# Eight opening loads handed to two queues by turns, in a fused adaLN attention and gMLP block

## The chip, the cores and the metric

One NeuronCore of one Trainium2 chip runs the whole program. The time is the device time of one execution, in microseconds (us); for each kernel the median of several executions is given. One further execution was taken with the hardware profiler, and all views of the trace belong to that one.

## The reference

The block has 2048 tokens of width 448, 16 heads of width 28, and a gMLP of inner width 896. Cut to what matters:

```python
mod = (silu(c) @ w_mod)                      # c is 1 x 448, w_mod is 448 x 2688
sa, ca, ga, sb, cb, gb = six rows of 448
h = layernorm(x) * (1 + ca) + sa
q, k, v = h @ wqkv                           # 448 x 1344
x = x + ga * (softmax(q k^T * 28**-0.5) v @ wo)
h = layernorm(x) * (1 + cb) + sb
z = gelu(h @ w_in); z1, z2 = z[:, :896], layernorm(z[:, 896:])
x = x + gb * ((z1 * (w_sp @ z2 + b_sp)) @ w_out)
```

Everything is in float32; nothing can be projected before `sa` and `ca` are there, and these need `silu(c)` and a third of `w_mod`.

## The kernel before, in words

The order on each engine is written out by hand: every engine runs its instructions strictly in the order in which the program issues them, and semaphores tie the engines together. The change lies in the first stage, the projections.

**The opening.** Tokens come in four groups of 512 (`load_x`, four tiles of 128 tokens each; line 175). Group 0 is loaded in three transfers (tile 0, tile 1, tiles 2 and 3), the others in one. `load_mod` (line 170) loads the first third of `w_mod`, the part for `sa` and `ca`, as four blocks of 112 rows, here called wm0 to wm3. `load_w("v", i)` loads the 448 rows of V's weights in blocks 0, 2, 1 (line 186) and 3; block 3 is 64 rows, loaded twice into the two halves of one tile (lines 87 and 88). So the opening's transfers stand in this order: c (line 202), three of x, wm0 to wm3, V's five, then group 1 of x. All of them are issued by SyncE (SP). ScalarE (ACT) issues transfers in one place only, the last stage, where it stores the output (line 1252).

**Completion counters.** The framework gives each transfer one of eight completion counters, by turns, in program order and over both issuing engines together. A transfer whose counter was used before waits, on the engine that issues it, until the earlier transfer with that counter has landed. The ninth transfer so waits for the first, the tenth for the second, and so on. The instruction that waits holds what stands behind it on its engine.

**What the first instructions do.** ACT loads its function table and computes `exp(-c)` into `ec` (line 214). VectorE (DVE) makes `silu` of it (lines 215 to 217). Behind these stand DVE's layer norm statistics of tiles 0 and 1 (lines 273, 274), their normalisation (284, after GpSimd's `rs`, lines 107 and 108), the statistics of tiles 2 and 3, then `mod_acc`: wm0 times its column of `silu` (233), wm1 added (235), the normalisation of tiles 2 and 3, wm2 added (235). `mod_last` (385) adds wm3 a column block at a time, TensorE (PE) sums over the rows (`pc`, line 391), and DVE writes the columns of `ca` and `sa` (397). With these ACT and DVE make the modulated, transposed h (409, 404, 84), and PE multiplies it with V's weights (`pv`, line 300). PE transposes the normalised tiles at line 351. Short matmuls that compute nothing (`pe_fill`, line 224) stand around those, to keep PE busy.

The first part of the weights of q and k (`load_w("a", i)`, lines 186, 87, 88) reuses the four buffers of wm0 to wm3. Later stages are attention (lines 572 to 618), the output projection, the gMLP's first matmul, the token mixing and the last matmul.

Of the kernel before, what the change touches and what calls it, by code (L numbers as in the profile page):

```python
# [33 lines left out]
def tile_adaln_mha_gmlp(ctx, tc, x, wqkv, wo, w_in, w_spT, b_sp, w_out, cT, w_mod, out):  # L34
    nc = tc.nc
    ctx.enter_context(tc.manual_schedule())
    pe, dve, act, pool, sp = nc.tensor, nc.vector, nc.scalar, nc.gpsimd, nc.sync
# [48 lines left out]
    def load_z(eng, dst, src):  # L86
        eng.dma_start(dst[0:64], src)
        eng.dma_start(dst[64:128], src)
# [73 lines left out]
    wms, xts, raws = {}, {}, {}  # L162
# [4 lines left out]
    def load_mod(pair, eng):  # L167
        for k in range(4):
            wms[pair, k] = e1.tile([112, 2, D], F32, name="wm", tag=("wm", "wm", "raw")[pair], bufs=4)
            eng.dma_start(wms[pair, k], w_mod[:, pair, k])  # L170

    def load_x(g, eng):
        xg = e1.tile([128, 4, D], F32, name="xg")
        for t0, t1 in ((0, 1), (1, 2), (2, 4)) if g == 0 else ((0, 4),):
            eng.dma_start(xg[:, t0:t1, :], x[g, :, t0:t1])
        for t in range(4):
            xts[4 * g + t] = xg[:, t, :]

# [3 lines left out]
    def load_w(kind, i, eng):  # L182
        c0, n, tag = PARTS[kind]
        raw = e1.tile([128, 2 * D], F32, name="raw", tag=tag, bufs=4)[:, :n]
        if i < 3:
            eng.dma_start(raw, wqkv[i * 128 : (i + 1) * 128, c0 : c0 + n])
        else:
            load_z(eng, raw, wqkv[384:448, c0 : c0 + n])
        raws[kind, i] = raw
# [11 lines left out]
    cc_t = e1.tile([112, 4], F32, name="cc_t", bufs=1)  # L201
    sp.dma_start(cc_t, cT)
    load_x(0, sp)
    load_mod(0, sp)
    for i in (0, 2, 1, 3):
        load_w("v", i, sp)
    load_x(1, sp)
    pool.memset(wv[64:128, 7, :].bitcast(F32), 0.0)
    pool.memset(wqk[64:128, 7, 0:896].bitcast(F32), 0.0)
# [240 lines left out]
    h_lo(3, dve)  # L450
    wv_lo(3, pool)
    load_x(2, sp)
    for i in (0, 2, 1, 3):
        load_w("b", i, sp)
# [7 lines left out]
    for i in (0, 2):  # L462
        qk_lo("a", i, dve)
    load_mod(1, sp)
    for a in pvs:
        v_copy(*a)
# [25 lines left out]
    for i in (0, 2, 1, 3):  # L492
        qk_part("b", i, dve)
    load_mod(2, sp)
    for g in range(1, NG):
        if g == 3:
# [878 lines left out]
```

## Time and profile before

| what | value |
|---|---|
| median of 3 executions | 1408.03 us (1407.81 to 1408.63) |
| the profiled execution | 1407.25 us |
| its span, first to last instruction | 1405.5 us |
| granted TensorE clock | 1.00 |
| DVE, ACT and GpSimd busy | 72%, 56%, 21% of the span |
| transfers issued by SP (queue q1) and by ACT (queue q10) | 181.88 MB and 3.84 MB |

The page of the profile gives the busy time of each engine, the span in 40 equal slices, the transfers, and the chain of work that ended last. The timeline gives single instructions: start, duration, engine, line, and in brackets how long the engine stood idle before it and what ended that. SPq and ACTq are the instructions by which SP and ACT issue transfers. Such an instruction is shown from the end of its wait on.

### The profile page before, as it was taken

Reading aid. Unit: us, or ns where it says so; the run is one execution under the profiler, and the core shown is the slowest. Engines: PE = TensorE matmul, PEld = TensorE weight load, DVE = VectorE, ACT = ScalarE, POOL = GpSimd, SP = SyncE. Lnnn points to the kernel's source line nnn. Section 1 sums busy time; section 2 is a strip of 40 time slices with the busy share of each in tenths; the row PEclk is TensorE's granted clock in tenths of the full one; section 3 lists DMA queues with packets and bytes.
Section 4 is the critical chain, followed back from the end, with each engine's and each line's share of the span. In section 5 each row is a group of like instructions: output and inputs, shape, how many; then the busy total and the mean of one; then the engine's idle time right before and its main releaser. Section 6 shows DMA issues by size and latency. Waiting matters only on the chain.

```text
span 1405.5 us, 20321 instructions
## 1 busy us (share of the span) xinstructions
PE 1393.3 (99%) x7164; PEld 981.2 (70%) x7164; DVE 1014.1 (72%) x1701; ACT 788.9 (56%) x1536; POOL 296.3 (21%) x284
## 2 busy tenths in 40 slices
PE   7999999999999999999999999999999999999999
PEld 7887655555555555555555554988998888888888
DVE  7798888888888888888888860751356655668574
ACT  4723677777777777777677779263234544434211
POOL 4234313122314243313200021100143430001000
PEclk9999999999999999999999999999999999999999
DMA  8564645555455556654422001534103333444453
GB/s 256 156 169 168 187 110 171 167 161 157 154 167 171 150 164 179 178 158 150 123 68 75 21 18 45 187 115 139 53 0 113 107 113 111 142 140 157 142 174 108
DMA packets 99377, 187.01 MB, mean 133 GB/s; under 512 B 17736, under 2 KB 29130, under 8 KB 96730
## 3 DMA queue, kind: packets, MB, share of 16 engines
q1 hardware_dynamic: 96846, 181.88, 43.0%
q10 hardware_dynamic: 2430, 3.84, 0.7%
q8 instruction: 56, 0.92, 0.3%
q14 instruction: 45, 0.37, 0.1%
HBM read 130.42 MB, written 50.46 MB: 129 GB/s over the span
## 4 chain that ended last, share of the span: by engine, by line
PE 96%; DMA 2%; DVE 1%; ACT 0%; issue 0%; SPq 0%; POOL 0%; DVEq 0%; ACTq 0%; POOLq 0%
PE st_ps L603 19%; PE o_ps L618 17%; PE mt L572 17%; PE acc L1143 6%; PE acc L1142 6%; PE acc L1144 6%; PE z_ps L1068 5%; PE z_ps L954 5%; PE pq L318 5%; PE wo_ps L824 3%; PE pv L300 2%; PE y_ps L1247 2%; PE y_ps L1248 2%; PE y_ps L1246 2%; PE tp L117 1%; DMA wm<-in_w_mod_dram 1%
## 5 line engine op out<-in xcount | busy, mean ns | idle before, releaser
L577 DVE TENSOR_REDUCE pm<-mt 128x1 f32<-128x512 f32 x1024 | 631.5, 682 | 110.0 <-PE mt L572 109.8
L607 ACT ACTIVATE P<-st_ps 128x512 f32<-128x512 f32 x1024 | 513.2, 621 | 150.0 <-PE st_ps L603 150.0
L603 PE MATMUL st_ps<-qst,kst 128*128 128x512 f32 x1024 | 407.5, 409 | 0.1
L572 PE MATMUL mt<-kst,qst 128*128 128x512 f32 x1024 | 402.1, 393 | 0.6 <-DVE pm L577 0.3
L603 PEld LDWEIGHTS st_ps<-qst,kst 128*128 128x128 f32 x1024 | 191.1, 187 | 151.4 <-issue 82.2
L618 PE MATMUL o_ps<-P,V 128*32 128x512 f32 x2048 | 247.5, 598 | 0.0
L572 PEld LDWEIGHTS mt<-kst,qst 128*128 128x128 f32 x1024 | 192.5, 188 | 32.9 <-DVE pm L577 2.3
L725 POOL TENSOR_TENSOR ws_raw<-ws_raw 128x512 f32<-128x512 f32 x80 | 102.9, 1287 | 282.8 <-DMA ws_raw<-in_w_spT_dram 270.4
L1030 ACT ACTIVATE wsp_h<-raw_sp 128x512 fp32r<-128x512 f32 x112 | 69.9, 631 | 154.4 <-PE acc L1144 103.6
L84 DVE TENSOR_TENSOR wsp_l<-raw_sp,wsp_h 128x512 fp32r<-128x512 f32 x112 | 82.0, 743 | 81.9 <-ACT wsp_h L1030 81.2
L618 PEld LDWEIGHTS o_ps<-P,V 128*32 128x32 f32 x2048 | 54.1, 109 | 123.5 <-issue 116.6
L1143 PE MATMUL acc<-wsp_l,heapA 128*128 128x512 f32 x224 | 87.4, 390 | 0.3 <-DVE wsp_l L84 0.2
L1142 PE MATMUL acc<-wsp_h,heapA 128*128 128x512 f32 x224 | 87.3, 390 | 0.0
L1144 PE MATMUL acc<-wsp_h,heapA 128*128 128x512 f32 x224 | 87.2, 389 | 0.0
L1143 PE MATMUL acc<-wsp_l,heapB 128*128 128x512 f32 x174 | 67.7, 389 | 0.0
L1144 PE MATMUL acc<-wsp_h,heapB 128*128 128x512 f32 x174 | 67.7, 389 | 0.0
L1142 PE MATMUL acc<-wsp_h,heapB 128*128 128x512 f32 x174 | 67.7, 389 | 0.0
L318 PE MATMUL pq<-heapD,heapD 128*128 128x512 f32 x196 | 61.9, 390 | 0.0
L1072 DVE BATCH_NORM_STATS2 stz<-z 128x6 f32<-128x448 f32 x32 | 19.9, 625 | 50.4 <-ACT z L1071 30.1
L1143 PEld LDWEIGHTS acc<-wsp_l,heapA 128*128 128x128 f32 x224 | 42.0, 188 | 9.6 <-DVE wsp_l L84 1.2
L1142 PEld LDWEIGHTS acc<-wsp_h,heapA 128*128 128x128 f32 x224 | 42.0, 188 | 9.0 <-DVE cD L1148 0.3
L1144 PEld LDWEIGHTS acc<-wsp_h,heapA 128*128 128x128 f32 x224 | 42.0, 188 | 8.8
(212 smaller groups left out, 1605.7 us busy)
## 6 DMA issues: line engine op xcount, KB each, us to landing
ws_raw<-in_w_spT_dram SPq DMA_DIRECT2D x160, 256.0 KB
ws_scr<-ws_raw SPq DMA_DIRECT2D x80, 256.0 KB
raw_sp<-ws_scr SPq DMA_DIRECT2D x80, 256.0 KB
kst<-qk_scr SPq DMA_DIRECT2D x45, 224.0 KB
qst<-qk_scr SPq DMA_DIRECT2D x45, 224.0 KB
raw_sp<-in_w_spT_dram SPq DMA_DIRECT2D x32, 256.0 KB
qk_scr<-qh SPq DMA_DIRECT2D x28, 256.0 KB
qk_scr<-ql SPq DMA_DIRECT2D x28, 256.0 KB
```

Source lines behind the costliest of these rows:

```text
L84: eng.tensor_tensor(out=dst, in0=a, in1=hi.bitcast(F32), op=ALU.subtract)
L318: pe.matmul(pq, wqk[:, b, m * 128 : (m + 1) * 128], hT[g][:, a, :], start=j == 0, stop=j == NST - 1)
L572: pe.matmul(mt, qst[h % 3][:, t * 128 : (t + 1) * 128], kst[h % 3][:, kb * 512 : (kb + 1) * 512], start=True, stop=True)
L577: dve.tensor_reduce(out=pms[h][:, t, kb : kb + 1], in_=mt, axis=AX.X, op=ALU.max)
L603: pe.matmul(st, kst[h % 3][:, kt * 128 : (kt + 1) * 128], qst[h % 3][:, qb * 512 : (qb + 1) * 512], start=True, stop=True)
L607: act.activation(p, st, AF.Exp, scale=SCALE)
L618: pe.matmul(otile[h][32 * qb : 32 * qb + 32, :], V[:, kt, h, :], ptiles.pop((u, qb)), start=kt == 0, stop=kt == NT - 1)
L725: pool.tensor_tensor(out=a, in0=a, in1=b, op=SUMS[i // 16][2])
L954: pe.matmul(ps_t, w1[:, b, f * 128 : (f + 1) * 128], h2T[g][:, a, :], start=j == 0, stop=j == NST - 1)
L1142: pe.matmul(acc[i], zh, hi, start=st == 0, stop=False)
L1143: pe.matmul(acc[i], zh, lo, start=False, stop=False)
L1144: pe.matmul(acc[i], zl, hi, start=False, stop=st == 7)
```

## The change

Every second transfer of the opening gets ACT as its issuing engine: tile 1 of x, wm0, wm2, and V's blocks 2 and 3 (six transfers, since block 3 has two). c, tile 0, tiles 2 and 3, wm1, wm3, V's blocks 0 and 1 and group 1 of x stay with SP. Line numbers stay as they are.

```diff
     def load_mod(pair, eng):
         for k in range(4):
...
-            eng.dma_start(wms[pair, k], w_mod[:, pair, k])
+            (act if pair == 0 and k % 2 == 0 else eng).dma_start(wms[pair, k], w_mod[:, pair, k])
     def load_x(g, eng):
...
-            eng.dma_start(xg[:, t0:t1, :], x[g, :, t0:t1])
+            (act if t0 == 1 else eng).dma_start(xg[:, t0:t1, :], x[g, :, t0:t1])
...
     for i in (0, 2, 1, 3):
-        load_w("v", i, sp)
+        load_w("v", i, act if i in (2, 3) else sp)
```

In the built program the order on PE, DVE and GpSimd is the same as before. ACT's program begins with the six transfers, and the table load and `exp(-c)` come behind them. The counters are given out in the same turns, over both engines in the order in which they issue. On ACT, tile 1, wm0 and wm2 wait for nothing; V's block 2 waits until c has landed, the first half of block 3 until wm0 has, and its second half until wm1 has, which SP issues.

## The prediction

> **What bounds the kernel now.** I read the page first, then busy time by stretch, then the chain of work that ended last in the first 70 us, then the engines' timelines there. From the page:
>
> ```profile
> PE 1393.3 (99%) x7164; PEld 981.2 (70%) x7164; DVE 1014.1 (72%) x1701; ACT 788.9 (56%) x1536; POOL 296.3 (21%) x284
> ```
>
> The busy times from 26 us up to the last 55 (window, length, busy time of PE, PEld, DVE, ACT, POOL, granted clock, DMA share, GB/s):
>
> ```profile
> 26.00:1350.00 1324.00, 1322.94 (x6804) 917.61 (x6805) 963.13 (x1607) 770.77 (x1503) 284.94 (x267) 1.00 0.43 130
> ```
>
> The reader is to see that from 26 us on PE never pauses: 1322.9 us of 1324. Nothing later can take in a delay. What shifts PE's start at 26 us shifts the end by as much, and nothing else in this change moves the end. So the question is the first 26 us. Their chain (start, duration, what):
>
> ```profile
> 4.00 10.50 DMA wm<-in_w_mod_dram
> ...
> 26.06 1.89 PE pv L300 x8
> ```
>
> The chain names wm3's transfer, but DVE's timeline says how much that transfer really costs:
>
> ```profile
> 2.62 1.01 DVE L215 TENSOR_SCALAR ec<-ec 112x4 f32<-112x4 f32 x1 [1.49 <-ACT ec L214]
> 3.67 0.18 DVE L216 RECIPROCAL ec<-ec 112x4 f32<-112x4 f32 x1
> 3.88 0.16 DVE L217 TENSOR_TENSOR silu<-cc_t,ec 112x4 f32<-112x4 f32 x1
> 4.33 0.63 DVE L273 BATCH_NORM_STATS2 st<-xg 128x6 f32<-128x448 f32 x1 [0.30 <-DMA xg<-in_x_dram]
> ...
> 11.19 1.15 DVE L235 SCALAR_TENSOR_TENSOR acc<-wm,silu,acc 112x896 f32<-112x896 f32 x1 [0.94 <-DMA wm<-in_w_mod_dram]
> ...
> 14.59 1.66 DVE L385 SCALAR_TENSOR_TENSOR acc<-wm,silu,acc 112x128 f32<-112x128 f32 x6 [0.34 <-DMA wm<-in_w_mod_dram]
> ...
> 17.69 0.16 DVE L397 TENSOR_SCALAR col_ca<-pc 128x1 f32<-128x1 f32 x1 [0.45 <-PE pc L391]
> ```
>
> From 4.33 us to 26 us DVE runs one chain, up to the parts of h that the `pv` at 26.06 needs. It waits for transfers only three times: 0.30, 0.94 and 0.34 us, 1.58 us in all. That is everything that earlier landings could ever give back. And the chain's head is `silu`, which waits for ACT's `ec`.
>
> **The change part by part.** *ACT's queue.* ACT's start before:
>
> ```profile
> 0.71 1.28 ACT L214 ACT_TABLE_LOAD   x1 [0.71 <-PEq L1363]
> 2.39 0.20 ACT L214 ACTIVATE ec<-cc_t 112x4 f32<-112x4 f32 x1 [0.39 <-DMA cc_t<-in_cT_dram]
> ```
>
> Now six issues stand ahead of both, and the last waits until wm1 has landed. Whether such a wait holds ACT's own work is shown where ACT issues transfers today, at the end:
>
> ```profile
> 1359.37 0.34 ACTq L1252 DMA_DIRECT2D out_dram<-x2l  x1
> 1359.75 1.68 ACT L1218 ACTIVATE uT<-cE 128x512 fp32r<-128x512 f32 x3 [8.15 <-DVE x2l L1251]
> ```
>
> ACT stood idle for 8.15 us until the issue's own input was there, and its next activation came behind it. So `ec` comes when wm1 has landed, the issue is out, and the table is loaded. Behind `ec` stands DVE's whole chain, and behind that PE.
>
> *When wm1 lands.* SP's timeline tells of landings, because each issue from the ninth on waits for one (8.10: all of group 0 of x; 9.44: wm0; 11.10: wm1; 12.93: wm2; DVE's row at 14.59: wm3):
>
> ```profile
> 1.18 1.36 SPq L175 DMA_DIRECT2D xg<-in_x_dram  x3
> 2.59 1.91 SPq L170 DMA_DIRECT2D wm<-in_w_mod_dram  x4
> ...
> 8.10 0.56 SPq L87 DMA_DIRECT2D raw<-in_wqkv_dram  x1
> 9.44 0.47 SPq L88 DMA_DIRECT2D raw<-in_wqkv_dram  x1
> 11.10 0.33 SPq L175 DMA_DIRECT2D xg<-in_x_dram  x1
> 12.93 2.75 SPq L186 DMA_DIRECT2D raw<-in_wqkv_dram  x3
> ```
>
> The four w_mod issues were out by 4.50 us, 10 us before wm3 landed, so these landings are set by bytes, not by issuing. The 16 DMA engines are full, as the same view by stretch shows:
>
> ```profile
> 0.00:2.00 2.00, 0.00 (x0) 0.00 (x0) 0.32 (x3) 1.28 (x1) 1.34 (x8) 1.00 0.03 1
> ...
> 7.00:13.00 6.00, 4.23 (x31) 4.04 (x30) 4.82 (x10) 0.71 (x3) 1.32 (x3) 1.00 1.03 237
> 18.00:20.00 2.00, 2.00 (x11) 1.86 (x10) 2.00 (x4) 1.57 (x3) 0.22 (x1) 1.00 1.05 381
> ```
>
> Sizes, from the list of issues:
>
> ```profile
> wm<-in_w_mod_dram SPq DMA_DIRECT2D x12, 392.0 KB
> raw<-in_wqkv_dram SPq DMA_DIRECT2D x3, 224.0 KB
> xg<-in_x_dram SPq DMA_DIRECT2D x2, 224.0 KB
> xg<-in_x_dram SPq DMA_DIRECT2D x1, 448.0 KB
> ```
>
> After the change wm1 is the last of 224 + 448 + 392 = 1064 KB on SP's queue. ACT's queue meanwhile carries 224 + 2 x 392 = 1008 KB (tile 1, wm0, wm2) and then 224 KB of V's block 2, which need c alone. If the engines serve both queues in turn, 2072 to 2296 KB are through when wm1 is. Before, 2072 KB (x and wm0 to wm2) were through at 12.9 us and 392 KB more at 14.55, so 2296 KB would be at 13.85. ACT can issue tile 1 from 0.71 us on (its row above), where SP issued its first tile of x at 1.18, so the first rows of x start 0.47 us earlier: 12.4 to 13.4 us. I take 12.8. So wm1, which before came second of four, now lands where wm2 did. The bound from below: all 2072 KB (2.12 MB) at the best of these rates, 381 GB/s, take 5.6 us. Before, almost nothing moved until 2.0 us; from 0.47 us sooner on that gives 7.1 us. From above: wm3's old place, 14.6.
>
> The page "DMA: Bandwidth & Descriptors" of the Trainium skill ("Issuing engines are not separate DMA queues") says that transfers from several engines run on the same 16 DMA engines and interleave, and that only issue time is saved. The share of 1.03 in the row above agrees with it; no row here shows two queues loading at once. By that page the 7.1 us would fall away as a bound.
>
> *From there to DVE.* The last issue takes 0.47 us (the row at 9.44) from 12.85 to 13.32, the table load 1.28 to 14.65, `ec` 0.20 to 14.87. DVE's first step took 1.01 us, because it ended with a GpSimd memset:
>
> ```profile
> 2.65 0.96 POOL L210 MEMSET V<- 128x1024 f32 x1
> ```
>
> That is long over now, so I take 0.16 us, as the small operation of line 397 has in the row at 17.69; bounds 0.16 and 1.01. The two steps to `silu` and the gaps take 0.46 as before (3.63 to 4.09). The statistics start at 15.5 instead of 4.33: **+11.2 us**. wm0 to wm3 have landed when they are asked for, so the waits of 0.94 and 0.34 go: **-1.3 us**. What is late next is PE's share in that chain:
>
> ```profile
> 4.98 4.08 PE L224 MATMUL wu<-ones,xg 128*128 128x128 f32 x18 [4.98 <-DVE st L273]
> 8.90 1.04 PE L351 MATMUL tp<-ident,xn 128*128 128x128 f32 x8
> 9.77 1.28 PE L224 MATMUL wu<-ones,xg 128*128 128x128 f32 x10
> 12.82 1.09 PE L351 MATMUL tp<-ident,xn 128*128 128x128 f32 x8 [1.77 <-DVE xn L284]
> ```
>
> The first 18 fills take 3.92 us up to the next row, 0.22 each; the transposes behind them 0.11, later fills 0.13. The fills wait for x alone, so they still run at 4 to 8 us, and then PE stands idle some 12 us until tile 0 is normalised. If it comes back at the slow pace, the 8 transposes and 10 fills, 18 matmuls too, take 3.9 us instead of 2.1. They start at 20.1 (8.90 + 11.2) and end at 24.0; the next transposes could start at 23.1 (12.82 + 11.2 - 0.94). So these come 0.9 later, and DVE's wait of 0.45 for the last `pc` grows by about **+0.7**. Bounds 0 and 0.9; I take 0.7, since the only long idle time in the trace, the start, was followed by the slow pace. By the Trainium skill's page "TensorE: Matmul & The Clock Gate" (Part 1), an idle time over about 3.4 us halves the clock; no later pause here shows it, and by that rule the 0.7 stands.
>
> *What stays hidden.* V's block 3 lands near 15 us and is used behind 28. Group 1 of x is now issued when tiles 2 and 3 have landed, but stands behind wm3 and V's blocks on SP's queue. The q and k weights still wait for wm0's to wm3's buffers, which come free about 10 us later, but then meet empty queues. Their earlier landing gives nothing (0 to -0.03), since DVE was busy for 7.97 of the last 8 us:
>
> ```profile
> 18.00:26.00 8.00, 7.36 (x35) 6.12 (x33) 7.97 (x9) 4.54 (x8) 6.22 (x5) 1.00 0.99 320
> ```
>
> SP's shorter queue gives nothing, since its issues waited for landings.
>
> **Sum:** 11.2 - 1.3 + 0.7 = +10.6 us, on the profiled execution (1407.25 us, span 1405.5) 1417.85, on the median, 0.78 above it, **1418.6 us** (+0.75%).
>
> **The rivals.** *Two queues move more bytes.* DMA engines that serve two queues might overlap them and reach 381 GB/s at once; then wm1 lands at 7.1 us and the loss is 10.6 - 5.7 = 4.9: 1412.9. For it: that rate is reached at 18 us, with one queue. Against: the share is already 1.03 with one.
>
> *wm1 lands last.* If ACT's rows are served first, wm1 waits for most of them and lands at wm3's old 14.6: +1.8, 1420.4 (1420.5 in the range, for the median's own spread).
>
> *Not slower: the wait stands in ACT's queue of transfers and not in ACT.* If ACT could go on to the table and `ec` while an issue waits, `silu` would come in time and earlier landings could remove the three waits: 1408.03 - 1.58 = 1406.4. It decides at `ec`: for no loss, `ec` must end by about 5.0 us (`silu` by 4.04 + 1.58, less 0.16 + 0.46). With ACT blocked that would need wm1 landed by 2.9 us, when it has barely been issued. The rows at 1359 us speak against it.
>
> **How the numbers follow.** Forecast 0.70, more bytes 0.17, wm1 last 0.08, not slower 0.05. The range runs from the first rival's time to the second's, 1412.9 to 1420.5. About 0.2% (2.8 us) is what a measurement can tell from no change. Not even the best case gains so much: faster 0.01, same 0.05, slower 0.94.
>
> **What would show it.** Right: ACT's table load near 13.4 us, behind six issues, of which the last two stand behind waits until about 9 and 12.8 us; DVE's `ec` idle 13 us or so; statistics at 15.5; no wait for wm; `pv` first at about 28; PE without a pause from 37. Wrong: a table load before 5 us, or a `pv` start that moves less than `silu` does.

## The result and the profile after

| what | before | after |
|---|---|---|
| median of 6 executions of each | 1407.91 us (1407.68 to 1408.63) | 1417.07 us (1416.90 to 1419.76) |
| ratio, after to before | | 1.0065, 95% interval 1.0054 to 1.0077 |
| the profiled execution, its span | 1407.25, 1405.5 us | 1417.01, 1415.2 us |

The changed kernel is 9.2 us slower. From the page of after, the busy times; and from its busy time by stretch, the row for 36 us up to the last stages (window, length, busy time of PE, PEld, DVE, ACT, POOL, granted clock, DMA share, GB/s):

```profile
PE 1396.3 (99%) x7164; PEld 983.5 (69%) x7164; DVE 1013.2 (72%) x1701; ACT 788.6 (56%) x1536; POOL 295.1 (21%) x284
```

```profile
36.00:1350.00 1314.00, 1312.63 (x6749) 907.45 (x6748) 953.92 (x1590) 768.83 (x1500) 281.76 (x266) 1.00 0.43 130
```

PE again never pauses once its long run has begun, now from about 36 us on. So the first 36 us are the place to look. ACT's timeline of after (start, duration, instruction, idle time before it and what ended that):

```profile
0.72 0.43 ACTq L175 DMA_DIRECT2D xg<-in_x_dram  x1
1.18 0.92 ACTq L170 DMA_DIRECT2D wm<-in_w_mod_dram  x2
3.06 0.35 ACTq L186 DMA_DIRECT2D raw<-in_wqkv_dram  x1
6.07 0.56 ACTq L87 DMA_DIRECT2D raw<-in_wqkv_dram  x1
10.98 0.48 ACTq L88 DMA_DIRECT2D raw<-in_wqkv_dram  x1
11.49 1.28 ACT L214 ACT_TABLE_LOAD   x1 [11.49 <-DMA raw<-in_wqkv_dram]
12.79 0.20 ACT L214 ACTIVATE ec<-cc_t 112x4 f32<-112x4 f32 x1
```

Six issues, then the table load, then `ec`. The last two issues stand behind waits, until 6.07 and 10.98. The bracket names `raw`, V's block 2, of which a piece came in at 11.44; but the table load starts 0.03 us after the last issue ends, and what held that issue until 10.98 is named by the chain of work that ended last:

```profile
2.12 8.84 DMA wm<-in_w_mod_dram
10.98 0.48 ACTq L88
11.49 1.28 ACT L214
...
34.55 1.90 PE pv L300 x8
```

The transfer that SP issued from 2.12 us on is wm1, and it landed at 10.96. DVE's timeline of after, with the same instructions as those shown of before:

```profile
13.03 0.17 DVE L215 TENSOR_SCALAR ec<-ec 112x4 f32<-112x4 f32 x1 [11.89 <-ACT ec L214]
...
13.52 0.62 DVE L273 BATCH_NORM_STATS2 st<-xg 128x6 f32<-128x448 f32 x1
...
19.27 1.15 DVE L235 SCALAR_TENSOR_TENSOR acc<-wm,silu,acc 112x896 f32<-112x896 f32 x1
21.03 0.94 DVE L284 TENSOR_SCALAR xn<-xg,mv,rs 128x448 f32<-128x448 f32 x2 [0.61 <-POOL rs L108]
...
23.06 1.67 DVE L385 SCALAR_TENSOR_TENSOR acc<-wm,silu,acc 112x128 f32<-112x128 f32 x6
...
26.16 0.16 DVE L397 TENSOR_SCALAR col_ca<-pc 128x1 f32<-128x1 f32 x1 [0.44 <-PE pc L391]
```

The statistics start at 13.52 instead of 4.33: **+9.19 us**. From there to `mod_last` (line 385) it is 9.54 us instead of 10.26: the waits of 0.94 and 0.34 for wm are gone, but a new one of 0.61 for GpSimd's `rs` has come: **-0.72 us**. PE's timeline of after:

```profile
16.82 1.97 PE L351 MATMUL tp<-ident,xn 128*128 128x128 f32 x8 [9.03 <-DVE xn L284]
18.57 2.34 PE L224 MATMUL wu<-ones,xg 128*128 128x128 f32 x10
21.60 1.10 PE L351 MATMUL tp<-ident,xn 128*128 128x128 f32 x8 [0.68 <-DVE xn L284]
...
34.55 1.90 PE L300 MATMUL pv<-wv,heapD 128*128 128x448 f32 x8 [0.57 <-DVE heapD L84]
```

The last `pv` of the stage starts at 34.55 instead of 26.06, +8.49, which the two DVE terms give (9.19 - 0.72 = 8.47). The profiled executions differ by 9.76 in all, and the medians by 9.16. What is beyond the stage, 0.7 to 1.3 us, comes up bit by bit later, where both kernels do the same work: DVE runs the same 1701 instructions in the same order, and they are 8.5 us late at 128 us of before, 10.7 at 804 us, near the end of attention, and 9.8 at the end. The kernel before itself ran from 1405.87 to 1412.02 us in 24 executions on one chip. So the shift of this `pv` is the sharper measure, and the experiments use it as "the stage's shift", beside the medians.

### The profile page after: what moved, and what is told of

Same layout as the page of the kernel before. It is cut to its first block, busy times and chain, and to the rows that moved or that the text cites. A ratio compares the mean times of both kernels' runs of the same rounds, so it can differ in the third digit from the quotient of the medians.

```text
span 1415.2 us, 20321 instructions
## 1 busy us (share of the span) xinstructions
PE 1396.3 (99%) x7164; PEld 983.5 (69%) x7164; DVE 1013.2 (72%) x1701; ACT 788.6 (56%) x1536; POOL 295.1 (21%) x284
## 4 chain that ended last, share of the span: by engine, by line
PE 96%; DVE 2%; DMA 1%; POOL 0%; ACT 0%; issue 0%; SPq 0%; ACTq 0%; DVEq 0%; POOLq 0%
PE st_ps L603 19%; PE o_ps L618 17%; PE mt L572 17%; PE acc L1143 6%; PE acc L1144 6%; PE acc L1142 6%; PE z_ps L1068 5%; PE z_ps L954 5%; PE pq L318 5%; PE wo_ps L824 3%; PE pv L300 2%; PE y_ps L1247 2%; PE y_ps L1248 2%; PE y_ps L1246 2%; PE tp L117 1%; DMA wm<-in_w_mod_dram 1%
```

## The experiments

Three theories stood against each other. **A**: the loss is the wait for a landing that stands in ACT's program ahead of the table load and `ec`. **B**: two queues loading at once make the transfers land later where they are needed. **C**: it is the time that ACT spends on issuing. Each edit is shown against the changed kernel, except where it says otherwise. The ratio in the table is an estimate from all executions, with its interval; it can differ from the quotient of the two medians by up to 0.0007.

| kernel | ACT issues | start of tile 0's statistics | stage's shift | median, its kernel before | ratio (95%) |
|---|---|---|---|---|---|
| after | all six | 13.52 | +8.49 | 1417.07, 1407.91 | 1.0065 (1.0054 to 1.0077) |
| e1_x_wm | tile 1, wm0, wm2 | 5.29 | +0.25 | 1410.38, 1408.59 | 1.0006 (0.9996 to 1.0017) |
| e2_v_only | V's three | 14.25 | +11.22 | 1418.11, 1408.59 | 1.0060 (1.0045 to 1.0076) |
| e3_last_half_sp | all but the last | 8.60 | +3.55 | 1412.13, 1408.59 | 1.0020 (1.0011 to 1.0029) |
| e4_ec_first | all six, behind `ec` | 4.10 | +3.34 | 1412.62, 1408.59 | 1.0025 (1.0015 to 1.0035) |
| e5_warm | all six, more fills | 14.03 | +12.46 | 1419.28, 1407.27 | 1.0083 (1.0069 to 1.0096) |
| e6_wait_alone | none | 10.32 | +5.27 | 1415.84, 1407.27 | 1.0056 (1.0038 to 1.0073) |
| e7_v_only_warm | V's three, more fills | 14.32 | +9.27 | 1416.93, 1407.27 | 1.0068 (1.0052 to 1.0083) |
| e8_ec_then_wm | wm0, wm2, behind `ec` | 4.36 | +4.21 | 1412.73, 1407.27 | 1.0036 (1.0023 to 1.0048) |

The two-queue part without a wait on ACT, **e1_x_wm**:

```diff
-        load_w("v", i, act if i in (2, 3) else sp)
+        load_w("v", i, sp)
```

> ACT issues tile 1 of x, wm0 and wm2, which wait for nothing; all of V's weights are SP's again. Theory A (the loss is ACT's wait for landings in its own program, ahead of exp(-c)): three issues end near 2.1 us, the table load near 3.4, ec near 3.65; the first statistics start when tile 0 of x lands, near 5.4, DVE then has no wait for wm, and the wm3 step starts at 14.4 against 14.59 before: about -0.2 us, a time of 1407.7, within 1 us of before. Rival B (two queues at once make the loads land later or hold each other up, and that is the loss): x and wm still come by two queues, so most of the loss stays, +6 to +9 us. Rival C (the loss is the issue time on ACT, 0.45 us each, and the table load behind it): +1.5 us.

ACT's and DVE's timelines of e1_x_wm:

```profile
1.18 0.92 ACTq L170 DMA_DIRECT2D wm<-in_w_mod_dram  x2
2.13 1.28 ACT L214 ACT_TABLE_LOAD   x1 [2.13 <-issue]
3.43 0.20 ACT L214 ACTIVATE ec<-cc_t 112x4 f32<-112x4 f32 x1
```

```profile
5.29 0.63 DVE L273 BATCH_NORM_STATS2 st<-xg 128x6 f32<-128x448 f32 x1 [1.04 <-DMA xg<-in_x_dram]
...
12.81 0.93 DVE L284 TENSOR_SCALAR xn<-xg,mv,rs 128x448 f32<-128x448 f32 x2 [0.61 <-POOL rs L108]
```

And the last `pv` of the stage, from PE's:

```profile
26.31 1.89 PE L300 MATMUL pv<-wv,heapD 128*128 128x448 f32 x8 [0.55 <-DVE heapD L84]
```

Three issues that wait for nothing delay `ec` by only 1.04 us (3.43 instead of 2.39), and `silu` (4.08, 0.16 long) is still there before the first tile of x. The statistics of tile 0 start 0.96 later than before, now that tile 1 and wm0 load beside that tile; the waits for wm are gone, the one for `rs` is there: +0.96 - 0.72 = +0.24, and the `pv` moved by +0.25. Two queues and 1.4 us of issuing on ACT cost nothing that the executions can tell: the interval of the ratio holds 1, though the medians lie 1.8 us apart, where less than 1 was expected. B and C fall as the cause of 8.5 us.

V's part alone, **e2_v_only**:

```diff
-            (act if pair == 0 and k % 2 == 0 else eng).dma_start(wms[pair, k], w_mod[:, pair, k])
+            eng.dma_start(wms[pair, k], w_mod[:, pair, k])
...
-            (act if t0 == 1 else eng).dma_start(xg[:, t0:t1, :], x[g, :, t0:t1])
+            eng.dma_start(xg[:, t0:t1, :], x[g, :, t0:t1])
```

> Only V's blocks 2 and 3 are issued by ACT; x and wm come by SP's queue alone, as before. Their counters make ACT wait for tile 0 of x, for tiles 2 and 3, and last for wm1. Theory A: wm1 lands at 11.1 as before, ec ends near 13.2, the statistics start near 13.8, the wm3 step near 23.2: +8.7 us in that stage, a time near 1416.6 to 1417. Rival B: nothing is loaded by two queues before wm3 is through, so no loss, 1408. Rival C: three issues and the table load, +1.5 us.

ACT's timeline of e2_v_only, then PE's and DVE's:

```profile
11.70 0.49 ACTq L88 DMA_DIRECT2D raw<-in_wqkv_dram  x1
12.22 1.28 ACT L214 ACT_TABLE_LOAD   x1 [12.22 <-DMA raw<-in_wqkv_dram]
```

```profile
22.33 1.97 PE L351 MATMUL tp<-ident,xn 128*128 128x128 f32 x8 [0.68 <-DVE xn L284]
```

```profile
26.68 0.16 DVE L397 TENSOR_SCALAR col_ca<-pc 128x1 f32<-128x1 f32 x1 [1.22 <-PE pc L391]
```

The wait is all here, with no x or w_mod issued by ACT: the statistics come 9.92 late, which with the -0.72 is +9.20. The stage moved by 11.22, so 2.0 us are new. They are PE's: its second eight transposes take 1.97 us here and 1.10 in after, and DVE waits 1.22 us for the first `pc`, a wait that after doesn't have. The term that the prediction put at +0.7 exists, and is larger, in this kernel.

The same transfers with one wait less on ACT, **e3_last_half_sp** (the second half of block 3 goes to SP, so ACT's last wait is the one for wm0):

```diff
     def load_z(eng, dst, src):
         eng.dma_start(dst[0:64], src)
-        eng.dma_start(dst[64:128], src)
+        (sp if eng is act else eng).dma_start(dst[64:128], src)
```

> As the changed kernel, but the second half of V's block 3 is issued by SP, so that the last landing for which ACT waits is wm0's (6.05 us in the trace of after) and not wm1's (10.96). Theory A: ACT's last issue ends at 6.6, the table load at 7.9, ec at 8.15, the statistics start at 8.7 instead of 13.5; waits for wm are still gone, GpSimd's second step is still late by 0.6: +3.7 us against before, 1411.6. Rival B: nothing changes in the two queues' loads, so +9 as in the changed kernel. Rival C: one issue less, +8.5.

ACT's and DVE's timelines of e3_last_half_sp:

```profile
5.98 0.56 ACTq L87 DMA_DIRECT2D raw<-in_wqkv_dram  x1
6.57 1.28 ACT L214 ACT_TABLE_LOAD   x1 [6.57 <-DMA wm<-in_w_mod_dram]
```

```profile
8.60 0.62 DVE L273 BATCH_NORM_STATS2 st<-xg 128x6 f32<-128x448 f32 x1
```

The table load follows the landing of wm0 as it followed that of wm1. 8.60 - 4.33 - 0.72 = 3.55, and the stage moved by 3.55. One issue of 0.48 us, moved to the other engine, is worth 4.9 us, since the wait for wm1 went with it.

All six issues behind the work that they held up, **e4_ec_first**:

```diff
     sp.dma_start(cc_t, cT)
+    ec = e1.tile([112, 4], F32, name="ec", bufs=1)
+    act.activation(ec, cc_t, AF.Exp, scale=-1.0)
     load_x(0, sp)
...
-    ec = e1.tile([112, 4], F32, name="ec", bufs=1)
-    act.activation(ec, cc_t, AF.Exp, scale=-1.0)
```

> As the changed kernel, all six transfers by ACT, but the table load and exp(-c) are issued ahead of them. Theory A: silu comes as before, DVE's chain runs as before; ACT still stands at the wait for wm1 until about 11 us, so the two small copies for the transposes, due at 7.6, come near 11.6, PE's transposes follow, and DVE's wait for the last pc grows from 0.45 by some 0.7: +0.5 to +1 us, about 1408.6. Rival B: the two queues carry the same loads, so +6 to +9 us. Rival C: the issues no longer stand ahead of ec, 0.

ACT's issue of tile 1 and DVE's statistics of tiles 0 and 1, from the timeline of e4_ec_first:

```profile
2.42 0.44 ACTq L175 DMA_DIRECT2D xg<-in_x_dram  x1
```

```profile
4.10 0.63 DVE L273 BATCH_NORM_STATS2 st<-xg 128x6 f32<-128x448 f32 x1
9.10 0.63 DVE L273 BATCH_NORM_STATS2 st<-xg 128x6 f32<-128x448 f32 x1 [4.16 <-DMA xg<-in_x_dram]
```

`silu` is in time again, and 5.2 of the 8.5 us are back. That is less than expected: tile 1 is issued 2.42 us into the run, when SP has already issued tiles 2 and 3 and is issuing w_mod, and it lands only at 9.08. DVE stands 4.16 us for it. Theory B, wrong for the changed kernel, is right here: what is needed first shares the engines with what is needed later.

The clock, by more fills, so that PE doesn't stand still while it waits for tile 0, **e5_warm**:

```diff
-    pe_fill(9, x1)
+    pe_fill(48, x1)
```

> The changed kernel with 48 instead of 9 fills ahead of the transposes, so that PE works on from 3.6 to about 16.5 us and its clock stays up. The prediction's third term (the slow pace costs 0.7 us): the last pv group of tiles 0 to 3 (34.55 us in after) starts 0.7 earlier, near 33.85. What the trace of after says against it (DVE's wait for the last pc is 0.44, before 0.45): no move, 34.55 within 0.1.

PE's timeline of e5_warm, then a row of its busy time by stretch (the third number from the end is the granted clock):

```profile
3.67 13.76 PE L224 MATMUL wu<-ones,xg 128*128 128x128 f32 x96 [3.67 <-DMA xg<-in_x_dram]
...
22.11 1.09 PE L351 MATMUL tp<-ident,xn 128*128 128x128 f32 x8 [2.57 <-DVE xn L284]
```

```profile
23.00:24.00 1.00, 1.00 (x8) 1.00 (x7) 0.96 (x3) 0.70 (x2) 0.00 (x0) 0.60 0.25 92
```

This missed: it was 4.0 us worse than after in the stage. 0.5 of that is the start of the statistics (wm1 landed at 11.47 here). The rest is the clock: it stayed full through the first transposes, where speed is worth nothing, and halved at 23.2 us, behind the later pause of 2.57 us, just ahead of `pc` and `pv`; it was 0.50 until 33.4. So the clock matters by where the slow microseconds fall.

The wait without anything else, **e6_wait_alone**: the kernel before, all transfers on SP, the table load at the start, and one tiny activation that reads wm1 ahead of `ec`. Its output is used nowhere. The edit is against the kernel before, and later lines move down by two.

```diff
     ec = e1.tile([112, 4], F32, name="ec", bufs=1)
+    seen = e1.tile([112, 4], F32, name="seen", bufs=1)
+    act.activation(seen, wms[0, 1][:, 0, 0:4], AF.Copy)
     act.activation(ec, cc_t, AF.Exp, scale=-1.0)
```

> The kernel before, all transfers by SP, with one small activation ahead of exp(-c) that reads four columns of wm1: ACT waits for wm1 by data, not by a counter, and no second queue loads anything. The table load stays at the start. Theory A (the wait ahead of exp(-c) is the loss): wm1 lands at 11.1, ec ends at 11.55, the statistics start at 12.1; with the wm waits gone (-1.3) and GpSimd's second step late by 0.6 the stage loses 7.0 us, and up to 2 more if PE's clock comes back late: 1415 to 1417. Rival B (two queues at once) and rival C (ACT's issue time): 0, 1408.

ACT's, SP's, DVE's and PE's timelines of e6_wait_alone:

```profile
9.49 0.20 ACT L215 ACTIVATE seen<-wm 112x4 f32<-112x4 f32 x1 [7.49 <-DMA wm<-in_w_mod_dram]
```

```profile
9.48 0.34 SPq L175 DMA_DIRECT2D xg<-in_x_dram  x1
```

```profile
10.32 0.62 DVE L275 BATCH_NORM_STATS2 st<-xg 128x6 f32<-128x448 f32 x1
```

```profile
31.33 1.89 PE L302 MATMUL pv<-wv,heapD 128*128 128x448 f32 x8 [0.57 <-DVE heapD L84]
```

Under B and C this edit costs nothing. It costs 10.32 - 4.33 - 0.72 = 5.27 us by the stage's sum, and the stage moved by 5.27. It is less than the 7.0 expected, because wm1 landed at 9.46 in this profile, where the same transfers in the same order landed it just before 11.10 in the profile of before (SP's row there). The size goes with the landing, as A says. The median moved by more than the stage (8.6 us, interval 5.3 to 10.3): the profiled execution is the shortest of four, 1411.57 us at a mean granted clock of 1.000, and the others took 1415.78 to 1418.77 at 0.998 to 0.995. Where in these the clock was lower, no trace shows.

The clock in e2, by the same means as in e5, **e7_v_only_warm**:

```diff
     # against e2_v_only
-    pe_fill(9, x1)
+    pe_fill(46, x1)
```

> The run with only V's blocks 2 and 3 by ACT, with 46 instead of 9 fills, so that PE works on until its transposes. There the last pv group of tiles 0 to 3 started at 37.28, and from DVE's wm3 step to the first pv it took 4.93 us against 2.92 in after, with the granted clock at 0.50 until 26.9. If the clock is the cause: 2.92 again, the last pv group near 35.3, the stage's loss 9.2 instead of 11.2. If something else in that run held PE: no move.

PE's timeline of e7_v_only_warm:

```profile
22.40 1.09 PE L351 MATMUL tp<-ident,xn 128*128 128x128 f32 x8 [2.34 <-DVE xn L284]
...
35.33 1.89 PE L300 MATMUL pv<-wv,heapD 128*128 128x448 f32 x8 [0.56 <-DVE heapD L84]
```

The statistics start where e2's do (14.32 and 14.25), the transposes take 1.09 us instead of 1.97, and the stage's shift falls from 11.22 to 9.27. 14.32 - 4.33 - 0.72 = 9.27: nothing is left over. The 2.0 us of e2 were PE's pace.

`ec` first, and only w_mod by two queues, **e8_ec_then_wm** (wm0 and wm2 by ACT, behind `ec`; x and V by SP):

```diff
     sp.dma_start(cc_t, cT)
+    ec = e1.tile([112, 4], F32, name="ec", bufs=1)
+    act.activation(ec, cc_t, AF.Exp, scale=-1.0)
...
-            (act if t0 == 1 else eng).dma_start(xg[:, t0:t1, :], x[g, :, t0:t1])
+            eng.dma_start(xg[:, t0:t1, :], x[g, :, t0:t1])
...
-        load_w("v", i, act if i in (2, 3) else sp)
+        load_w("v", i, sp)
...
-    ec = e1.tile([112, 4], F32, name="ec", bufs=1)
-    act.activation(ec, cc_t, AF.Exp, scale=-1.0)
```

> A candidate: table load and exp(-c) stay first on ACT, then ACT issues wm0 and wm2 alone; x, wm1, wm3 and all of V's weights stay with SP. No wait stands on ACT. Theory A: silu as before, tile 0 lands near 4.1, wm1 and wm3 land before DVE asks; of the 1.58 us of waits 0.2, 0.34 and 0.94 less 0.61 (GpSimd's second step takes its place) go: the last pv group of tiles 0 to 3 near 25.2 instead of 26.06, -0.9 us, which the times can hardly tell from no change. Rival B: two queues at once cost several us, 1412 or more.

DVE's timeline of e8_ec_then_wm, tile 2's statistics, then wm1 and the first `pc`:

```profile
11.19 0.63 DVE L273 BATCH_NORM_STATS2 st<-xg 128x6 f32<-128x448 f32 x1 [3.16 <-DMA xg<-in_x_dram]
...
14.24 1.15 DVE L235 SCALAR_TENSOR_TENSOR acc<-wm,silu,acc 112x896 f32<-112x896 f32 x1 [0.91 <-DMA wm<-in_w_mod_dram]
...
19.88 0.16 DVE L397 TENSOR_SCALAR col_ca<-pc 128x1 f32<-128x1 f32 x1 [0.88 <-PE pc L391]
```

This was meant to be the faster version, and it is 4.2 us slower in the stage. wm0 and wm2 now load beside tiles 2 and 3, which land at 11.16 instead of 8.08; DVE waits 3.16 for them and once more for wm1, and PE, idle meanwhile, goes over to the slow pace as it comes back, which is DVE's 0.88. The Trainium skill's page "DMA: Bandwidth & Descriptors" ("Issuing engines are not separate DMA queues") says that transfers of several engines share the 16 DMA engines and interleave. This run and e4 agree with it. The page counts the saved issue time as the only effect; here the interleaving also cost 3.1 us on the transfer that was needed first. No version faster than the kernel before was found, and 1.58 us was all that one could have gained.

Last, both kernels again, unchanged, two profiles of each: whether the spread of the executions lies in the opening, and how well the landings repeat.

> The kernel before, unchanged, profiled once more. Of its 24 executions beside the first experiments, 12 had a mean granted clock of 1.000 and took 1405.9 to 1409.8 us, five had 0.996 and took 1411.3 to 1412.0. Theory D: the lower clock lies in the opening, where PE pauses, and delays the last pv of the stage: at a clock of 1.000 it starts at 26.1 plus or minus 0.3 us, at 0.996 some 3.5 us later. Rival: the lower clock lies later in the run, and the pv starts at 26.1 at either clock.

> The kernel before, unchanged, a third profile, with the same question: by theory D the last pv of the stage starts at 26.1 us at a mean granted clock of 1.000 and some 3.5 us later at 0.996; by the rival at 26.1 at either.

> The changed kernel, unchanged, profiled once more. Four of its six executions had a mean granted clock of 0.996 and took 1416.9 to 1417.1 us, two had 1.000 and took 1419.4 and 1419.8. Theory D: those two ran the opening's matmuls at the slow pace from the start, so that no change of the clock was recorded; at 0.996 the last pv of the stage starts near 34.55 us, at 1.000 some 2.5 us later, with slow transposes and slow pc. Rival: it starts near 34.55 at either clock, and the 2.5 us come in attention.

> The changed kernel, unchanged, a third profile, with the same question: by theory D the last pv of the stage starts near 34.55 us at a mean granted clock of 0.996 and some 2.5 us later at 1.000; by the rival near 34.55 at either. When wm1 lands (10.96 in the first profile) is read from ACT's last issue; by the spread seen so far it lies between 9.5 and 12 us.

The last `pv` of the stage, from PE's timelines of e9_before_again and of e12_after_third:

```profile
26.42 1.90 PE L300 MATMUL pv<-wv,heapD 128*128 128x448 f32 x8 [0.57 <-DVE heapD L84]
```

```profile
34.78 1.89 PE L300 MATMUL pv<-wv,heapD 128*128 128x448 f32 x8 [0.57 <-DVE heapD L84]
```

In e10 it starts at 25.99, in e11 at 34.72. Three profiles of before so give 25.99 to 26.42, three of after 34.55 to 34.78: the mean shift is 8.53 us, and it repeats to some 0.3. But the kernels before ran at a clock of 1.000 both times (1407.12 and 1405.99 us) and those after at 0.996 both times (1416.50 and 1418.39), so theory D and its rival were not told apart. One half of D can be read all the same: in all three profiles of after the granted clock is 0.50 for 10.24 us of the opening (11.40 to 21.64 in the first) and 1.00 from there to 1400 us, and this stretch alone makes the mean 0.996. The two executions of after differ by 1.89 us at the same clock, with the stage's end 0.06 apart; that much of the spread, at least, comes later. Why it comes stays open.

## Why the prediction was right, step by step

**The mechanism was right.** ACT held its table load and `ec` behind an issue that waited for wm1, and the whole chain moved by that. e6 shows that the wait alone does it, e1 that the rest of the change does not, e3 that the size follows the landing waited for. The rival that the wait stands in ACT's queue of transfers and not in ACT is refuted by ACT's timeline of after: no table load before 11.49. The other two rivals, wm1 at 7.1 and at 14.6, are refuted by its landing at 10.96.

**+11.2 was +9.19.** The step "2072 KB were through at 12.9 us, so wm1 lands at 12.8" was off by 1.84 us; the rest of that chain was right to 0.15 (issue 0.48, table 1.28, `ec` 0.20, DVE's first step 0.17 as taken, and the statistics 0.08 behind the start of `silu`). The bytes show why. Busy time by stretch, of before and then of after; the last number is GB/s:

```profile
0.00:4.00 4.00, 0.00 (x0) 0.00 (x0) 1.63 (x6) 1.49 (x2) 2.89 (x9) 1.00 0.43 112
...
0.00:12.90 12.90, 6.15 (x37) 5.99 (x38) 7.89 (x20) 2.10 (x5) 5.13 (x13) 1.00 0.82 215
```

```profile
0.00:4.00 4.00, 0.39 (x2) 0.42 (x3) 0.32 (x3) 0.00 (x0) 2.89 (x9) 1.00 0.51 156
...
0.00:10.96 10.96, 4.18 (x18) 3.91 (x18) 0.32 (x3) 0.00 (x0) 2.89 (x9) 1.00 0.85 234
```

When wm2 landed in before, 215 x 12.9 = 2.77 MB had moved, not the 2.12 MB (2072 KB) up to it: part of wm3 and V was already in when the last piece of wm2 came. A landing is the last of 16 pieces, and these don't end together: the trace has the pieces of wm2 in before at 10.22 us (the first), 11.86 (the fifteenth) and 12.84 (the last), so one piece alone came a whole microsecond behind the others. Those of wm1 in after lie at 10.20, 10.92 and 10.96. When wm1 landed in after, 234 x 10.96 = 2.56 MB had moved. At before's rate from 4 us on (2.33 MB in 8.9 us, 0.261 MB/us), those 0.21 MB less are 0.8 us of the 1.94 us between 12.9 and 10.96. The two queues moved 0.18 MB more in the first 4 us (156 instead of 112 GB/s), 0.7 us, of which the prediction had counted 0.47 us for the earlier first issue; against that it had allowed some 0.4 us for V's block 2 (12.8 instead of 12.4). After 4 us the rate was 0.279 MB/us, the remaining 0.5 us. It was not chance. ACT's rows of the two further profiles of after show the issue that waits for wm1 at 11.15 and 11.22 us. So wm1 lands about where it did before (11.10, and 11.52 and 11.34 in the two further profiles of before), although it now has wm2 beside it.

**-1.3 was -0.72.** The two waits did go. What the step left out is GpSimd's second `rs` (line 108). From the timelines of before and of after:

```profile
10.42 0.72 POOL L108 TENSOR_TENSOR rs<-rs,mhalf 128x2 f32<-128x2 f32 x1
```

```profile
19.41 1.59 POOL L108 TENSOR_TENSOR rs<-rs,mhalf 128x2 f32<-128x2 f32 x1
```

In before it ran while DVE waited for wm1; now DVE runs `acc` (line 235) at that time, the step takes 0.87 us longer and ends 0.58 us behind that `acc`, and DVE then waits 0.61 us for it. The wait that was taken away had covered another. The same 0.61 stands in e1's row, where nothing else of the stage moved by more than 1 us. In all 14 profiles the step takes 0.72 us where DVE stands still beside it (before, e8, e9, e10) and 1.59 where `acc` runs beside it (the other ten). That the two engines get in each other's way is argued from this overlap; it wasn't tried by itself.

**+0.7 was 0.** The slow pace came, as PE's rows of after show: the 8 transposes and 10 fills took from 16.82 to 20.91, 4.1 us where 3.9 was forecast. But the step began the chain at 20.1, taking the 8.90 of before and adding the shift. In before PE came to these transposes late, because its fills ran until then; in after they started as soon as tile 0 was normalised. That slack took in the slow pace, and DVE's last wait for `pc` was 0.44 instead of 0.45. e2 shows the term at 2.0 us where the slow pace lasts until the `pc`, and e7 takes it away again.

**The sum:** 9.2 - 0.7 + 0 = 8.5 in the stage where +10.6 was forecast; the medians give +9.2, 1.5 us below the forecast of 1418.6. In the stage the miss of 2.1 us is -2.0 from the start of the statistics, most of it wm1's landing, +0.6 from `rs` and -0.7 from PE's pace; 0.7 us came back later in the run. It is not chance alone: from 128 to 804 us the three profiles of after fall 1.0 to 2.3 us further behind the first of before, while e9 and e10, the two further ones of before, keep their distance to 0.2. The cause of this drift stays open.

## What to carry to other kernels

Before an issue of a transfer is given to an engine that computes, look which completion counter it gets and whose landing it must wait for: the price is that landing, and it falls on whatever stands behind the issue on that engine (here six issues, 2.7 us of ACT's time, cost 8.5, and 4.9 of them go if the one issue of 0.48 us that waits longest is left with SP). If such issues must stand there, put the engine's first computation ahead of them, and keep what is needed first alone on the DMA engines; a second queue added no speed here where they were full (from 4 to 10.9 us, 262 to 293 GB/s in the eight profiles with x and w_mod on two queues, 256 to 295 in the six with one), it changed who was served first. When a wait disappears, ask which other engine's step it had hidden.

## What the runs showed of the hardware that was not expected

- The same transfers in the same order can land some 2 us apart: wm1 at 9.46 in e6, at 11.1 to 11.5 in three profiles of before, whose SP issues the same list. It is the last pieces that differ: the first of wm1's 16 pieces comes at 8.77 in e6 and at 8.31 to 8.67 in those three, the last at 9.46 and at 11.09 to 11.51. Durations on the other engines mostly repeat to a few hundredths.
- PE's pace halves behind a pause, but not at one length of it: it came back slow after idle times of 9.03 (after), 8.38 (e2) and 3.95 us (e3), and halved 0.3 us into the new work after 3.28 (e8) and 1.1 us after 2.57 (e5), while 2.58 (e1) and 2.34 (e7) did nothing. What repeats is the length of the stretches at a clock of 0.50: 3.41 us in e8, 3.42 in e3, 10.24 in after, e5, e11 and e12, 13.65 in e2, that is one, three and four times 3.41. The Trainium skill's page "TensorE: Matmul & The Clock Gate" (Part 1) tells of a free-running window of about 3.4 us; these lengths agree with it. Of the 3.41 us ahead of the halving in e5, PE had been idle for 2.3. In after the clock was full again after 4.8 us of work, in e2 only after 9.4; how much work in a window it takes, these runs don't settle.
- GpSimd's second `rs`, on 128x2 elements, takes 0.72 us where DVE stands still and 1.59 where DVE runs `acc` on 112x896 beside it.
